# K and V of a head group projected together by token, 160 columns, in a two-block attention kernel

## The chip, the cores and the metric

The kernel runs on one core of a Trainium2 chip. A core has five engines with instruction streams of their own: TensorE (PE in the profile, its weight loads PEld), VectorE (DVE), ScalarE (ACT), GpSimd (POOL) and SyncE (SP), the last of which here only issues DMAs. Matmuls write to PSUM; ACT and DVE move their results to SBUF. The metric is device microseconds for one execution: the median of three runs was 2835.52 us (2830.86 to 2836.12).

## The reference

Four layers follow each other on 2048 tokens of 640 numbers: A, B, A, B, each with a layer norm ahead and a residual around it. Both A layers use the same weights. Layer A is attention in four segments of 512 tokens with a running memory; it has 32 heads of 20.

```python
def _A_ref(x, wq, wk, wv, wo, beta):
    H, Dh, N, L = 32, 20, 4, 512
    q, k, v = x @ wq, x @ wk, x @ wv          # as heads and segments
    phi = lambda t: jnp.where(t > 0, t + 1.0, jnp.exp(t))
    M, z = 0, 0
    for s in range(N):
        logits = einsum('bhqd,bhkd->bhqk', qs, ks) * Dh ** -0.5 + mask   # causal
        a_dot = softmax(logits) @ vs
        pq = phi(qs)
        a_mem = (pq @ M) / (pq @ z + 1e-06)
        o = g * a_mem + (1.0 - g) * a_dot      # g = sigmoid(beta), per head
        pk = phi(ks)
        M = M + einsum('bhld,bhle->bhde', pk, vs)
        z = z + pk.sum(tokens)
    return o @ wo

x = x + _A_ref(_layernorm(x), ...)
x = x + _B_ref(_layernorm(x), ...)
x = x + _A_ref(_layernorm(x), ...)
x = x + _B_ref(_layernorm(x), ...)
```

Layer B is a recurrent attention over 64 steps of 32 tokens. The change does not touch it.

## The kernel before, in words

`layer_A` works through 32 *groups*: four segments n, and in each eight groups G of four heads. A head takes 32 rows or columns of a tile of 128, 20 of them used. For each group:

- `proj_q` and `proj_k` (lines 276 and 295) project by feature: five matmuls, one for each 128 rows of the 640 inputs, with 128 padded weight columns as weights and 512 tokens moving. The result is Q^T or K^T, [128 head rows, 512 tokens]. ACT copies it to SBUF as `a_qT` and `a_kT`; for K it adds `C.krow`, which sets rows 20 and 21 of each head to 1. Those two rows carry the negated row maximum through the second score product.
- `proj_v` (line 306) projects by token: for each of four tiles of 128 tokens five matmuls with the tokens as weights and 80 weight columns moving. ACT copies the result to `vaug`, whose column 20 of each head is 1, so that the sum of the softmax comes out of the same product.
- `s_round` (lines 366 to 375) makes scores with the mask, `a_S`, and DVE takes the negated row maxima `a_nm`. `negmax_rows` (POOL) and `q_with_max` put them into rows 20 and 21 of the next Q^T, `a_q`. `t_round` (407 to 412) makes the transposed scores `a_T` with the maximum already taken off; ACT takes exp to `a_PT`, and POOL zeroes what lies above the diagonal.
- `pv` (424) multiplies the probabilities with `vaug`; ACT copies out `a_osb`; `norm` divides and puts the group's columns into `Onat`.
- `phi_k` (318 to 324), in segments 0 to 2: PE transposes `a_kT` back to tokens (`a_KN`), ACT takes exp (`a_EK`), POOL clips it to 0..1, DVE adds the positive part of `a_KN` from PSUM: `a_phik`. `state` (333 to 353) uses the memory for `a_NUM` in segments 1 to 3 and adds this group's product `a_UP` of `a_phik` and `vaug` to it.
- `out_stage_a` and `out_stage_b` (248 to 265) project finished token tiles of the segment before with `wo` (`a_YP`), in groups 2 to 5 of segments 1 to 3 and after the last group.

The groups are software pipelined: while group g has its scores made, `t_round` works on a group some three half groups behind, `proj_q` and `proj_k` on g + 1, `pv` on g - 2. The loop at the end of `layer_A` says at which (half, round) each piece is called. The framework's scheduler then lays out each engine's stream from that; an engine takes its stream in order.

Two PSUM pools couple the engines. `a_psx` has three buffers for the score tiles `a_S` and `a_T`, each freed by the reduce on DVE or the exp on ACT. `a_pg` has two buffers for everything else: QP, KP, VP, KN, NUM, UP, YP, Q2, PV and the transposes take turns, and each waits for the copy that frees the buffer two tiles before it.

Weights: `load_A_weights` pads `wq` and `wk` from a staging copy in the first A layer, stores the padded forms to DRAM, and the second A layer loads them from there. `wv` is loaded as it is.

Of the kernel before, what the change touches and what calls it, by code (L numbers as in the profile page):

```python
# [28 lines left out]
D = 640  # L29
# [8 lines left out]
def alloc_consts(tc, ctx):  # L38
    cp = ctx.enter_context(tc.tile_pool(name="consts", bufs=1))
    C = Consts()  # L40
    C.pool = cp
    C.identb = cp.tile([128, 128], BF16, name="c_identb")
    C.mhalf = cp.tile([128, 1], F32, name="c_mhalf")
    C.negu = cp.tile([128, 2, 128], BF16, name="c_negu")
    C.krow = cp.tile([128, 1], F32, name="c_krow")
    C.bdmask = cp.tile([128, 128], F32, name="c_bd")
    W = AWeights()
    W.g = cp.tile([128, 32], F32, name="a_g")
    W.omg = cp.tile([128, 32], F32, name="a_omg")
    return C, W  # L50


def build_consts(nc, tc, C):
    with ExitStack() as tctx:
# [15 lines left out]
        krows = tp_.tile([128, 4, 2], F32, name="c_krows")  # L70
        nc.vector.tensor_copy(krows[:], identf[:].rearrange("p (j s) -> p j s", s=32)[:, :, 20:22])
        nc.vector.tensor_reduce(out=C.krow[:], in_=krows[:].rearrange("p j s -> p (j s)"), axis=AX.X, op=ALU.add)
# [68 lines left out]
def load_A_weights(nc, W, A_wq, A_wk, A_wv, A_wo, padded, stage):  # L141

    first = not padded
    for nm, src, pad in (("wq", A_wq, W.wq), ("wk", A_wk, W.wk)):
        if first:
            raw = stage[nm]
            nc.gpsimd.memset(pad[:, :, :, 20:32], 0.0)
            nc.vector.tensor_copy(pad[:, :, :, 0:20], raw.rearrange("p c (h d) -> p c h d", d=20))
        else:
            nc.sync.dma_start(pad[:].rearrange("p c h s -> p (c h s)"), padded[nm])  # L150
    nc.sync.dma_start(W.wv[:], A_wv.rearrange("(c p) n -> p c n", p=128))
    nc.sync.dma_start(W.wo[:], A_wo.rearrange("(c p) n -> p c n", p=128))


def keep_padded(nc, tc, W, padded):
    for nm, pad in (("wq", W.wq), ("wk", W.wk)):
        padded[nm] = tc.dram_tile([128, NCH * 1024], BF16, name=f"a_{nm}_home")
        nc.sync.dma_start(padded[nm], pad[:].rearrange("p c h s -> p (c h s)"))


def layer_A(nc, tc, C, W, x_src, x_dst, src_is_bf16, nseg=4, out_bf16=False, xb_dst=None, load_w=None, side_loads=None):
# [7 lines left out]
    with ExitStack() as ctx:  # L169
# [5 lines left out]
        W.wk = pw.tile([128, NCH, 32, 32], BF16, name="a_wk_pad")  # L175
        W.wv = pw.tile([128, NCH, D], BF16, name="a_wv")
# [28 lines left out]
        vaug = [stm.tile([128, 4, 4, 32], BF16, name=f"a_vaug{i}") for i in range(3)]  # L205
        phik = [ste.tile([128, 4, 4, 32], BF16, name=f"a_phik{i}") for i in range(2)]
        for i in range(3):
            nc.gpsimd.memset(vaug[i][:], 0.0)
            nc.gpsimd.memset(vaug[i][:, :, :, 20:21], 1.0)
# [79 lines left out]
        def proj_k(g):  # L289
            n, G = divmod(g, 8)  # L290
            xnT = SEG[n]["xnT"]
            wkG = W.wk[:, :, 4 * G:4 * G + 4, :].rearrange("p c h s -> p c (h s)")
            KP = pg.tile([128, 512], F32, name="a_KP", tag="pg")
            for c in range(NCH):
                nc.tensor.matmul(KP[:], lhsT=wkG[:, c, :], rhs=xnT[:, c, :], start=(c == 0), stop=(c == NCH - 1))
            kT = qp4.tile([128, 512], BF16, name="a_kT")
            nc.scalar.activation(out=kT[:], in_=KP[:], func=ACT.Identity, bias=C.krow[:, 0:1], scale=1.0)
            GS[g]["kT"] = kT

        def proj_v(g):  # L300
            n, G = divmod(g, 8)
            xnT = SEG[n]["xnT"]
            VP = pg.tile([128, 4, 80], F32, name="a_VP", tag="pg")
            for tt in range(4):
                for c in range(NCH):
                    nc.tensor.matmul(VP[:, tt, :], lhsT=xnT[:, c, 128 * tt:128 * tt + 128], rhs=W.wv[:, c, 80 * G:80 * G + 80],
                                     start=(c == 0), stop=(c == NCH - 1))
            va = vaug[g % 3]
            nc.scalar.copy(va[:, :, :, 0:20], VP[:].rearrange("p t (j s) -> p t j s", s=20))
            GS[g]["va"] = va  # L310

        def phi_k(g):
# [3 lines left out]
            KN = pg.tile([128, 4, 128], BF16, name="a_KN", tag="pg")  # L316
            for tt in range(4):
                nc.tensor.transpose(KN[:, tt, :], GS[g]["kT"][:, 128 * tt:128 * tt + 128], C.identb[:])
            KNv = KN[:].rearrange("p t (j s) -> p t j s", s=32)[:, :, :, 0:20]
# [757 lines left out]
def full_kernel(tc, A_x, A_wq, A_wk, A_wv, A_wo, A_beta, B_x, B_mem0, B_Wq, B_Wk, B_Wv, B_Wo, B_seg_len, out, layers="ABAB"):  # L1077
    nc = tc.nc
    with ExitStack() as ctx:
# [8 lines left out]
        stage = {nm: t_[:, NCH - 1, 0:NCH * D].rearrange("p (c n) -> p c n", c=NCH) for nm, t_ in (("wq", WB.wq), ("wk", WB.wk))}  # L1088
        for nm, src in (("wq", A_wq), ("wk", A_wk)):
# [77 lines left out]
```

## Time and profile before

| what | value |
| --- | --- |
| median of 3 runs | 2835.52 us (2830.86 to 2836.12) |
| the profiled execution's own time | 2836.99 us |
| its span, first to last instruction | 2835.3 us |
| mean granted clock of TensorE | 0.979 |
| first layer A, groups in flight | about 30 to 410 us of the span |
| second layer A, groups in flight | about 1445 to 1830 us |
| PE, DVE, ACT, POOL busy | 2667.9, 1676.5, 1567.3, 702.8 us |

The profile is of one execution. "Busy" is the time in which an engine has an instruction in flight; for PE the ends of matmuls are modelled and hold a pipeline tail, so differences between starts say more than durations. In a line of the timeline the columns are start, duration, engine, source line, operation, output and inputs, shapes, count, and in brackets the idle time before it with what ended it. In a group's line the figures after the bar are busy time and the mean duration of one in ns, then the idle time before it.

### The profile page before, as it was taken

How to read it: one execution, taken by the hardware profiler on the slowest of the kernel's cores; microseconds unless marked ns; L12 is line 12 of the kernel's file. 1: busy time of each engine (PE TensorE's matmuls, PEld its weight loads, DVE VectorE, ACT ScalarE, POOL GpSimd, SP SyncE). 2: the span in 40 equal slices, each digit the busy share in tenths (PEclk: the TensorE clock that was granted, in tenths of full speed). 3: DMA queues.
4: the chain of work that ended last, by engine and by line, in shares of the span. 5: the costliest groups of instructions: out<-in, count | busy, mean ns of one | idle time of the engine just before them, and what ended most of it. 6: DMA issues, size and time to landing. Idle time of an engine off the chain costs nothing.

```text
span 2835.3 us, 147285 instructions
## 1 busy us (share of the span) xinstructions
PE 2667.9 (94%) x65736; PEld 1703.8 (60%) x65736; DVE 1676.5 (59%) x4554; ACT 1567.3 (55%) x3516; POOL 702.8 (25%) x1634
## 2 busy tenths in 40 slices
PE   5899998999999999999979999889999999999998
PEld 2455555666666666666635555556666666666665
DVE  5778864555555555555568878545555555555554
ACT  3777773555555555544448777545555555555443
POOL 3456651111111111111135666411111111111110
PEclk9999999999999999999989999899999999999999
DMA  6110135212221222121130111531211111211110
GB/s 215 53 43 23 39 127 134 44 40 47 44 44 42 43 46 45 41 41 31 31 114 20 57 48 34 174 94 41 43 39 41 41 41 42 43 40 38 39 26 20
DMA packets 322956, 156.54 MB, mean 55 GB/s; under 512 B 245776, under 2 KB 311056, under 8 KB 319248
## 3 DMA queue, kind: packets, MB, share of 16 engines
q1 hardware_dynamic: 320880, 136.63, 19.1%
q8 instruction: 514, 8.42, 1.3%
q10 hardware_dynamic: 1440, 10.49, 1.0%
q14 instruction: 122, 1.00, 0.1%
HBM read 95.65 MB, written 51.38 MB: 52 GB/s over the span
## 4 chain that ended last, share of the span: by engine, by line
PE 54%; DVE 4%; ACT 3%; DMA 2%; issue 1%; POOL 1%; SPq 0%; ACTq 0%; DVEq 0%; POOLq 0%
PE b_OPS L105 7%; PE b_tail L105 4%; PE b_Ka L105 4%; PE b_Qa L105 4%; PE b_Kb L105 4%; PE b_Qb L105 4%; PE b_Va L105 3%; PE b_Vb L105 3%; PE b_SP L105 3%; PE b_OTP L105 2%; PE b_PTP L105 2%; PE b_vtail L105 2%; PE b_OPSd L105 2%; DVE a_nm L375 2%; PE a_QP L276 1%
## 5 line engine op out<-in xcount | busy, mean ns | idle before, releaser
L105 PEld LDWEIGHTS <-b_HX 128*32 128x32 bf16 x15360 | 435.9, 97 | 338.7 <-issue 16.5
L375 DVE TENSOR_REDUCE a_nm<-a_S 128x2 f32<-128x1024 f32 (+3 forms) x512 | 403.7, 811 | 95.1 <-PE a_T L407 71.3
L105 POOL TENSOR_TENSOR b_Pm<-b_E,b_rs 128x96 bf16<-128x96 bf16 x128 | 63.5, 496 | 1446.1 <-ACT b_Vth L105 1082.8
L410 ACT ACTIVATE a_PT<-a_T 128x1024 bf16<-128x1024 f32 (+1 forms) x384 | 340.7, 891 | 51.7 <-PE a_T L407 46.8
L105 PE MATMUL b_OPS<-b_wo,b_OTsb 128*32 128x320 bf16 x8192 | 309.9, 301 | 10.3 <-issue 7.3
L105 PEld LDWEIGHTS <-b_OTsb 128*32 128x32 bf16 x8192 | 201.5, 97 | 97.7 <-DVE b_OTsb L105 25.9
L412 POOL TENSOR_SCALAR_AFFINE_SELECT a_PT<-a_PT 128x256 bf16<-128x256 bf16 (+1 forms) x384 | 198.6, 520 | 235.2 <-ACT a_PT L410 234.0
L105 DVE CAST b_HX<-b_MT 128x8 bf16<-128x8 f32 x372 | 63.7, 172 | 278.5 <-PE b_MT L105 273.4
L105 ACT CAST b_msb<-b_OPS 128x64 bf16<-128x64 f32 x378 | 69.3, 256 | 238.0 <-PE b_OPS L105 238.0
L105 ACT CAST b_kq<-b_Kb 128x512 bf16<-128x512 f32 x128 | 75.0, 586 | 202.4 <-PE b_Kb L105 202.4
L105 DVE COPY b_KT<-b_TPak 128x128 bf16<-128x128 bf16 x128 | 28.8, 225 | 227.2 <-PE b_TPak L105 227.2
L105 PE MATMUL b_Va<-b_wv,b_HX 128*32 128x512 bf16 x2520 | 160.7, 380 | 0.0
L105 PE MATMUL b_Vb<-b_wv,b_HX 128*32 128x512 bf16 x2520 | 160.0, 379 | 0.0
L407 PE MATMUL a_T<-a_q,a_kT 32*128 32x512 bf16 (+3 forms) x1024 | 139.6, 307 | 21.4 <-DVE a_nm L375 14.9
L105 PE MATMUL b_Ka<-b_wk,b_HX 128*32 128x512 bf16 x2520 | 159.0, 379 | 0.0
L105 PE MATMUL b_Kb<-b_wk,b_HX 128*32 128x512 bf16 x2520 | 158.9, 379 | 0.0
L105 PE MATMUL b_Qa<-b_wq,b_HX 128*32 128x512 bf16 x2520 | 158.9, 379 | 0.0
L105 PE MATMUL b_Qb<-b_wq,b_HX 128*32 128x512 bf16 x2520 | 158.9, 379 | 0.0
L105 PEld LDWEIGHTS <-b_kq 128*128 128x128 bf16 x2080 | 116.9, 98 | 69.0 <-ACT b_kq L105 54.8
L105 DVE TENSOR_SCALAR b_kq<-b_Qa 128x512 bf16<-128x512 f32 x128 | 88.5, 692 | 116.7 <-PE b_Qa L105 114.0
L105 DVE CAST b_OTsb<-b_OTP 128x160 bf16<-128x160 f32 (+1 forms) x384 | 122.5, 373 | 40.5 <-PE b_OTP L105 40.3
L105 PE MATMUL b_vtail<-b_wv,b_TX 128*32 128x256 bf16 x2880 | 138.9, 271 | 8.0 <-issue 4.8
(196 smaller groups left out, 5745.1 us busy)
## 6 DMA issues: line engine op xcount, KB each, us to landing
b_QKd<-b_tu SPq DMA_DIRECT2D x128, 128.0 KB
b_tl<-b_QKd SPq DMA_DIRECT2D x128, 128.0 KB
b_wv<-in_B_Wv_dram SPq DMA_DIRECT2D x10, 1024.0 KB
b_wo<-in_B_Wo_dram SPq DMA_DIRECT2D x16, 640.0 KB
b_VTd<-b_vt SPq DMA_DIRECT2D x256, 32.0 KB
b_Vth<-b_VTd SPq DMA_DIRECT2D x512, 16.0 KB
b_XO<-xres SPq DMA_DIRECT2D x256, 30.0 KB
b_wk<-in_B_Wk_dram ACTq DMA_DIRECT2D x5, 1024.0 KB
```

The lines of the kernel that those rows point to most:

```text
L105: r = f(*a, **k)
L276: nc.tensor.matmul(QP[:], lhsT=wqG[:, c, :], rhs=xnT[:, c, :], start=(c == 0), stop=(c == NCH - 1))
L375: nc.vector.tensor_reduce(out=nm[:, qc, 2 * pr:2 * pr + 2], in_=X[:, :, o:o + w_], axis=AX.X, op=ALU.max, negate=True)
L407: nc.tensor.matmul(Y[:, e, o:o + w_], lhsT=kT[rows, 128 * kc:128 * kc + 128], rhs=q2[rows, 128 * kc:512], start=True, stop=True, tile_posi ...
L410: nc.scalar.activation(out=PT[:, :, b:b + width], in_=Y[:, :, 0:width], func=ACT.Exp, scale=SC)
L412: nc.gpsimd.affine_select(out=dv, in_=dv, pattern=[[0, 2], [0, diag], [1, 128]], compare_op=ALU.is_ge, fill=0.0, base=0, channel_multiplie ...
```

## The change

K is no longer projected by feature. `proj_kv` projects K and V of a group by token with one weight tile of 160 columns (80 of K, 80 of V), in two halves of two token tiles each, for the next group. Each half has ten matmuls and two ACT copies: K into `Kn`, a tile of SBUF whose columns 20 and 21 of each head were set to 1 once, and V into `vaug`. `k_turn` makes K^T from `Kn` by four transposes and one ACT copy. `phi_k` no longer transposes K back; it reads `Kn` from SBUF, and is called earlier. V of group g is now made in group g - 1, so `vaug` has a fourth buffer. The weights of K and V are interleaved once, from staged copies on DVE, and stored to DRAM in that form for the second A layer. `C.krow` goes.

```diff
-    nc.sync.dma_start(W.wv[:], A_wv.rearrange("(c p) n -> p c n", p=128))
+    if first:
+        nc.gpsimd.memset(W.wq[:, :, :, 20:32], 0.0)
+        nc.vector.tensor_copy(W.wq[:, :, :, 0:20], stage["wq"].rearrange("p c (h d) -> p c h d", d=20))
+        for i, nm in enumerate(("wk", "wv")):
+            nc.vector.tensor_copy(W.wkv[:, :, :, 80 * i:80 * i + 80], stage[nm].rearrange("p c (g n) -> p c g n", n=80))
+    else:
+        nc.sync.dma_start(W.wq[:].rearrange("p c h s -> p (c h s)"), padded["wq"])
+        nc.sync.dma_start(W.wkv[:].rearrange("p c g n -> p (c g n)"), padded["wkv"])
...
-        vaug = [stm.tile([128, 4, 4, 32], BF16, name=f"a_vaug{i}") for i in range(3)]
+        vaug = [stm.tile([128, 4, 4, 32], BF16, name=f"a_vaug{i}") for i in range(4)]
+        Kn = [stm.tile([128, 4, 4, 32], BF16, name=f"a_Kn{i}") for i in range(2)]
+        for i in range(2):
+            nc.gpsimd.memset(Kn[i][:], 0.0)
+            nc.gpsimd.memset(Kn[i][:, :, :, 20:22], 1.0)
...
-        def proj_k(g):
+        def proj_kv(g, hf):
             n, G = divmod(g, 8)
             xnT = SEG[n]["xnT"]
-            wkG = W.wk[:, :, 4 * G:4 * G + 4, :].rearrange("p c h s -> p c (h s)")
-            KP = pg.tile([128, 512], F32, name="a_KP", tag="pg")
-            for c in range(NCH):
-                nc.tensor.matmul(KP[:], lhsT=wkG[:, c, :], rhs=xnT[:, c, :], start=(c == 0), stop=(c == NCH - 1))
+            KV = pg.tile([128, 2, 160], F32, name="a_KV", tag="pg")
+            for t2 in range(2):
+                tt = 2 * hf + t2
+                for c in range(NCH):
+                    nc.tensor.matmul(KV[:, t2, :], lhsT=xnT[:, c, 128 * tt:128 * tt + 128], rhs=W.wkv[:, c, G, :],
+                                     start=(c == 0), stop=(c == NCH - 1))
+            for dst, o in ((Kn[g % 2], 0), (vaug[g % 4], 80)):
+                nc.scalar.copy(dst[:, 2 * hf:2 * hf + 2, :, 0:20], KV[:, :, o:o + 80].rearrange("p t (j s) -> p t j s", s=20))
+            GS[g]["va"] = vaug[g % 4]
+
+        def k_turn(g):
+            KT_ = pg.tile([128, 4, 128], BF16, name="a_KT", tag="pg")
+            for tt in range(4):
+                nc.tensor.transpose(KT_[:, tt, :], Kn[g % 2][:, tt, :, :].rearrange("p j s -> p (j s)"), C.identb[:])
             kT = qp4.tile([128, 512], BF16, name="a_kT")
-            nc.scalar.activation(out=kT[:], in_=KP[:], func=ACT.Identity, bias=C.krow[:, 0:1], scale=1.0)
+            nc.scalar.copy(kT[:], KT_[:].rearrange("p t k -> p (t k)"))
             GS[g]["kT"] = kT
-
-        def proj_v(g):
-            ...
         def phi_k(g):
             n = g // 8
             if n > nseg - 2:
                 return
-            KN = pg.tile([128, 4, 128], BF16, name="a_KN", tag="pg")
-            for tt in range(4):
-                nc.tensor.transpose(KN[:, tt, :], GS[g]["kT"][:, 128 * tt:128 * tt + 128], C.identb[:])
-            KNv = KN[:].rearrange("p t (j s) -> p t j s", s=32)[:, :, :, 0:20]
+            KNv = Kn[g % 2][:, :, :, 0:20]
...
         proj_q(0)
-        proj_k(0)
+        proj_kv(0, 0)
+        proj_kv(0, 1)
+        k_turn(0)
...
-                    if k == (0, 2) and g + 1 < NGR:
-                        proj_k(g + 1)
-                    if k == (1, 0) and g < NGR:
-                        proj_v(g)
+                    if k == (0, 2):
+                        if g < NGR:
+                            phi_k(g)
+                        if g + 1 < NGR:
+                            proj_kv(g + 1, 0)
+                    if k == (1, 0) and g + 1 < NGR:
+                        proj_kv(g + 1, 1)
                     if k == (1, 1):
                         if 0 <= g - 2 < NGR:
                             pv(g - 2)
-                        if g < NGR:
-                            phi_k(g)
+                        if g + 1 < NGR:
+                            k_turn(g + 1)
...
-        for nm, src in (("wq", A_wq), ("wk", A_wk)):
+        for nm, src in (("wq", A_wq), ("wk", A_wk), ("wv", A_wv)):
             nc.sync.dma_start(stage[nm], src.rearrange("(c p) n -> p c n", p=128))
```

More of the change, by code (lines that the diff above doesn't have):

```diff
@@ L174, in layer_A @@
         W.wq = pw.tile([128, NCH, 32, 32], BF16, name="a_wq_pad")
-        W.wk = pw.tile([128, NCH, 32, 32], BF16, name="a_wk_pad")
-        W.wv = pw.tile([128, NCH, D], BF16, name="a_wv")
+        W.wkv = pw.tile([128, NCH, 8, 160], BF16, name="a_wkv")
         pxT = pool("a_xnT", 2)
```

30 lines of the change are left out of this document (5 added, 25 removed).

## The prediction

> **What bounds the kernel now.** I read the page's table of engines first, then stretches of the two A layers, then the timeline of single groups, then the groups of instructions for prices. In the table TensorE (PE) is the only engine near its span.
>
> ```profile
> PE 2667.9 (94%) x65736; PEld 1703.8 (60%) x65736; DVE 1676.5 (59%) x4554; ACT 1567.3 (55%) x3516; POOL 702.8 (25%) x1634
> ```
>
> The change touches layer A alone, so the second view is busy time by stretch, here the two A layers (columns: stretch, length, busy time of PE, PEld, DVE, ACT, POOL, granted clock, DMA share, GB/s). There PE is busy 300.88 of 325 us, but ACT and DVE stand at 252: three engines hand work round, and the clock is close to full.
>
> ```profile
> core 0: us, PE busy (x) PEld busy (x) DVE busy (x) ACT busy (x) POOL busy (x), PEclk, DMA share, GB/s
> 85.00:410.00 325.00, 300.88 (x3927) 170.02 (x3926) 252.94 (x510) 252.47 (x407) 195.49 (x394) 0.97 0.15 50
> 1425.00:1830.00 405.00, 360.63 (x4626) 205.13 (x4615) 300.84 (x607) 287.55 (x462) 222.16 (x451) 0.94 0.21 66
> ```
>
> The third view is the timeline of one group (four heads) of the second A layer, from its PV block to its Q projection.
>
> ```profile
> 1642.14 1.17 PE L424 MATMUL a_PV<-a_vaug,a_PT 128*128 128x32 bf16 x40
> 1643.15 0.38 PE L318 MATMUL a_KN<-c_identb,a_kT 128*128 128x128 bf16 x4
> 1643.37 0.28 PE L366 MATMUL a_S<-c_negu,c_identb 128*128 128x128 bf16 x2
> ...
> 1643.73 0.44 ACT L321 ACTIVATE a_EK<-a_KN 128x320 f32<-128x320 bf16 x1
> ...
> 1644.26 0.45 POOL L322 TENSOR_SCALAR a_EK<-a_EK 128x320 f32<-128x320 f32 x1 [0.29 <-ACT a_EK L321]
> ...
> 1644.75 0.49 DVE L324 SCALAR_TENSOR_TENSOR a_phik<-a_KN,a_EK 128x320 bf16<-128x320 bf16 x1
> ...
> 1645.30 0.40 PE L348 MATMUL a_UP<-a_vaug,a_phik 128*128 128x128 bf16 x4 [0.19 <-DVE a_phik L324]
> 1645.53 1.24 PE L276 MATMUL a_QP<-a_xnT,a_wq_pad 128*128 128x512 bf16 x5
> ```
>
> See the feature map as a relay: PE transposes K, ACT takes exp, POOL clips, DVE adds, and only then may PE do UP. Busy times of PE hold a modelled pipeline tail, so I count PE by start to start. That of the K and V projections:
>
> ```profile
> 1661.99 1.25 PE L295 MATMUL a_KP<-a_xnT,a_wk_pad 128*128 128x512 bf16 x5
> ...
> 1663.18 0.39 PE L407 MATMUL a_T<-a_q,a_kT 32*128 32x512 bf16 x2
> ...
> 1663.50 0.89 PE L306 MATMUL a_VP<-a_wv,a_xnT 128*128 128x80 bf16 x20
> ...
> 1664.22 0.39 PE L366 MATMUL a_S<-c_negu,c_identb 128*128 128x256 bf16 x2
> ```
>
> KP takes 1.19 us, VP 0.72 (36 ns a matmul), KN 0.22 (1643.15 to 1643.37, 55 ns each). The pace of the groups is read from the same instruction of successive groups:
>
> ```profile
> 1653.91 0.44 ACT L427 COPY a_osb<-a_PV 128x336 f32<-128x336 f32 x1
> 1666.13 0.44 ACT L427 COPY a_osb<-a_PV 128x336 f32<-128x336 f32 x1
> ...
> 1746.69 0.44 ACT L427 COPY a_osb<-a_PV 128x336 f32<-128x336 f32 x1
> 1757.56 0.44 ACT L427 COPY a_osb<-a_PV 128x336 f32<-128x336 f32 x1
> ```
>
> With the one at 1643.40: 10.51 us without an output stage, 12.22 with one (YP), 10.87 in the last segment, where there is no feature map; in segment 0 it is 9.78 (1497.73 to 1507.51).
>
> **PE work, per group.** Removed: KP 1.19, VP 0.72, and KN 0.22 in the 48 groups of segments 0 to 2. Added: 20 matmuls of 160 columns and 4 transposes. No row has 160 columns; 128 take 55 ns (KN), 320 take 0.136 us (YP: 1656.05 to 1656.73, 0.68 for five), so by columns 68 ns, 1.36 us in all, bounds 1.10 and 2.7. The first half stands between row-tiled matmuls like KP and keeps KP's switch of about 0.11 us. KT costs what KN did, 0.22. Balance: 2.13 becomes 1.69, minus 0.44 us; in segment 3, which had no KN, minus 0.22.
>
> Weighed against that: the Trainium skill, "TensorE: Matmul & The Clock Gate", section "Back-to-back issue gap", says that pairs of weight load and matmul sustain about 81 ns at 128 columns and 131 at 512. An estimate between them is 85 ns for 160 columns, 0.34 us more a group, and would make it 22 us over 64 groups: no gain. The trace's 55 and 36 ns speak against it here.
>
> **ACT work.** Prices come from the groups of instructions (busy, mean ns):
>
> ```profile
> L297 ACT ACTIVATE a_kT<-a_KP,c_krow 128x512 bf16<-128x512 f32 x64 | 44.0, 688 | 28.8 <-PE a_KP L295 28.5
> L391 ACT CAST a_q<-a_Q 128x512 bf16<-128x512 f32 x64 | 38.3, 598 | 0.4 <-PE a_Q L388 0.3
> L309 ACT CAST a_vaug<-a_VP 128x320 bf16<-128x320 f32 x64 | 27.3, 427 | 0.7 <-PE a_VP L306 0.6
> L105 ACT CAST b_PTa<-b_PTP 128x160 bf16<-128x160 f32 x256 | 62.3, 295 | 99.8 <-PE b_PTP L105 99.8
> ```
>
> Removed 688 + 427; added four copies of 160 elements at 295 and one kT copy as a_q, 598: 665 ns more a group. But ACT's instructions overlap: two b_PTa back to back take 0.49 us, so one holds ACT 0.19; the others hold it about 0.12 less than their means. So +0.33 us a group, bounds 0.33 and 0.665. EK keeps its price (read from SBUF: no ACT row of this size; I take 443 ns again, bounds plus or minus 0.1, on no path below).
>
> **What moves.** In the changed order KV half 1 stands where KP stood, half 2 where VP stood, KT where KN stood, and UP right behind NUM. EK is done behind the second KV copies, a group ahead, so the relay is off the path. In its place ACT does osb and then the kT copy before UP, YP and the next S. From PV's start (no YP): NUM waits for osb, 1.75 (as now: 1643.89 less 1642.14). kT follows osb's 0.33 of ACT: 1.57 to 2.17, so UP, whose PSUM buffer (two in that pool) is the one KT used, starts at 2.22 instead of 3.16. S 512 follows at 2.66 (now 2.18), T 512 at 2.77, QP at 3.09 instead of 3.39. What is late next: the S reduce on DVE, which now stands behind upm and a_rd and starts at 3.45 instead of 3.21; it frees T's buffer at 4.66, which puts Q2 at 5.05; qT, EQ, exp and q2 on ACT then let KV start at 6.88 instead of 7.20 (1649.34). From KP to PV now 3.32, less 0.42: PV comes again at 9.8 instead of 10.5, minus 0.65 to 0.70. After KV the S reduce sets a floor: S at 1504.22 to PV at 1506.25 is 2.03 us whatever V costs, so V's shorter price is worth nothing.
>
> With YP: QP waits for the first YP to be added on DVE, and that waits for the same S reduce: 5.5 now and after. So only KV's 0.42 is left. Segment 0: T 512 waits for osb, the reciprocal and the S 256 reduce now as then (2.58), UP comes behind it; QP is at 3.47 against 3.39; 0.42 less 0.08 is 0.35. Segment 3: there was no KN in the way, YP now waits for kT (2.22, now 1.75): plus 0.46 against 0.42, nothing with YP; about 0.3 without.
>
> **Starts.** The first S needs 20 matmuls, copies, KT and the kT copy in series instead of KP and kT: cold, at 0.14 us for 160 columns (five 512s took 2.13), 2.7 + 0.3 + 0.6 + 0.6 against 2.1 + 0.7, plus 1.4 us a layer; less V's 0.9 later, which is under the S reduces. In the first layer one more staged weight (0.82 MB) lies ahead of x on SP's queue, and the store of the wide weights (1.64 MB) ahead of x's third tile, at about 0.3 MB/us; but the weight copies now run before x lands: from minus 1 to plus 4, I take plus 1.2. The second layer loads 0.5 MB less; POOL's extra memsets of 2 us lie in its waits there. DVE loses 12 of 490 ns a phik at most: nothing taken. B is unchanged.
>
> **Sum.** 16 groups without YP in segments 1 and 2 at 0.65: 10.4. 16 with YP at 0.42: 6.7. 16 of segment 0 at 0.35: 5.6. Segment 3, 8 at 0.3: 2.4. The last group's V, gone from each tail: 1.4. Together 26.5, less 4.0 for the starts: minus 22.5. The profiled execution took 2836.99 us around its 2835.3 span, 1.5 above the median of 2835.52; against the median, 2813 to 2814.5. I say 2814.
>
> **Rivals.** (1) *More comes back.* Segment 3 is 1.35 us faster than 12.22 though KN and UP are only 0.45 of PE: 0.9 us hang on the relay. If PE's 0.44 (0.22) and the 0.26 that T 512 waits ahead of UP (1644.72 to 1645.30 against 0.32) both return in all groups: 24.6 + 12.5 + 1.4 - 4 = 34, 2801; with the whole 0.9 in 32 groups, 49: 2786. Against it: the S reduces. (2) *ACT becomes the bound, slower.* Place: osb and kT ahead of UP, S and YP. Start to start (four exps of 0.90, two of 0.48, nine others of 0.31 to 0.59) ACT is taken for 8.5 of 10.5 us in a group with a transpose, 8.8 after. If its 2 us of idle time, nearly all waits for PE's Q, don't shrink, each group grows by 0.33: plus 21 plus 4 - 1.4, 2859; it decides against the change once kT is over 0.8 us later than 2.17, that is, if copies into strided K and V rows don't overlap (plus 0.33 more) and exp queues ahead of osb. For it: from 1643.40 to 1646.2 ACT has hardly a gap. A third of it, 0.1 us a group, gives 2845. (3) *Weight loads bound the 160-column matmuls:* at 85 ns instead of 68, plus 0.34 in 64 groups, 2836; the rows of 36 and 55 ns speak against it. (4) *The starts eat it*, if x's later tiles wait out both stores, plus 10 each: 2834.
>
> **Numbers.** Forecast 0.48 (its own range 2804 to 2824), (1) 0.22, (2) 0.18, (3) 0.06, (4) 0.06. The range reaches from 2794, inside (1), to 2845, a third of (2). Within 0.2% (5.7 us, about what this kernel's measurements can tell) lie (3), (4) in part: 0.09; faster 0.73, slower 0.18.
>
> **What would show it.** KV halves of 0.68 to 0.79 us start to start; no idle time ahead of UP from a_phik; osb to osb 9.8, 11.8, 9.4 and 10.9 in the four kinds of group; the first S about 1.5 us later behind QP. It is wrong if PE waits for a_kT ahead of S or UP by over 0.5 us, if KV costs over 0.8 a half, or if the YP groups gain as much as the others.

## The result, and the profile after

The changed kernel takes 2807.69 us, the median of four runs (2805.53 to 2811.1); the kernel before, in four runs beside it, 2833.19 (2826.18 to 2836.12). The ratio is 0.9916, with a 95% interval of 0.99 to 0.9933: 0.8% faster, 25.5 us. The profiled execution took 2809.46 us around a span of 2807.7, at a mean granted clock of 0.984 (2836.99, 2835.3 and 0.979 before).

The table of engines of the changed kernel, and then busy time in the two A layers (columns as before: stretch, length, PE, PEld, DVE, ACT, POOL, granted clock, DMA share, GB/s):

```profile
PE 2637.4 (94%) x65416; PEld 1720.3 (61%) x65480; DVE 1688.6 (60%) x4553; ACT 1589.9 (57%) x3708; POOL 701.5 (25%) x1645
```

```profile
85.00:410.00 325.00, 296.03 (x3858) 182.71 (x3883) 255.13 (x509) 263.03 (x491) 194.42 (x390) 0.97 0.16 54
1425.00:1830.00 405.00, 359.29 (x4836) 224.14 (x4869) 313.64 (x627) 302.44 (x568) 223.85 (x467) 0.96 0.24 76
```

PE lost 30 us of busy time and ACT gained 23. That fits a sum of 25 us, and it says nothing of where the time came from. The pace of the groups tells more, read from the same copy (osb) of successive groups. The timeline of the changed kernel, second A layer; the pairs are segment 0, a YP group, and a group without YP:

```profile
1479.13 0.44 ACT L421 COPY a_osb<-a_PV 128x336 f32<-128x336 f32 x1
1488.16 0.44 ACT L421 COPY a_osb<-a_PV 128x336 f32<-128x336 f32 x1
...
1552.60 0.44 ACT L421 COPY a_osb<-a_PV 128x336 f32<-128x336 f32 x1
1565.09 0.44 ACT L421 COPY a_osb<-a_PV 128x336 f32<-128x336 f32 x1
...
1621.71 0.44 ACT L421 COPY a_osb<-a_PV 128x336 f32<-128x336 f32 x1
1631.66 0.46 ACT L421 COPY a_osb<-a_PV 128x336 f32<-128x336 f32 x1
```

In the steady groups, segment 0 is at 9.03 us (9.78 before), the groups without YP at 9.95 (10.52), and the YP groups at **12.49, longer than the 12.22 of before**. Taken over all 62 intervals from osb to osb of the two layers, and the stretches ahead, between and behind, the two profiled executions differ like this (us, after minus before):

| part | forecast | measured |
|---|---|---|
| segment 0 (12 intervals) | -5.6 | -8.3 |
| segments 1 and 2 without YP (14) | -9.1 (14 at 0.65) | -9.2 |
| iterations (2, 7) and (3, 0), twice | -1.3 (one of each pair a no-YP group) | **-9.4** |
| segments 1 and 2 with YP (16) | -6.7 | **+4.7** |
| segment 3 (16) | -2.4 | +1.2 |
| up to the first osb | +2.6 | **-3.8** |
| from the last osb of A to the first of the next A | +1.4 less 0.7 | -0.8 |
| behind the last osb of the second A | -0.7 | -2.1 |
| sum | -22.5 | -27.7 |

Iterations are numbered (segment, group) as the loop runs; PV and osb belong to the group two earlier, and an interval has the name of the iteration in which it begins. The forecast sum is some 5 us from this one, but three parts miss it by 6 to 11 us each, and in both directions. The experiments are about those.

Two agreements in the table are in part luck. The 14 intervals without YP match the forecast only in their sum: the four at (2, 0) and (2, 1) gained 0.32 to 0.57 us where 0.65 was said, and the eight of segment 1 gave 7.0 of the 9.2 us; why those gained more was not tested. And the granted clock has a part that the table hides. In seven intervals it was 0.75 to 0.96 before and 1.00 after: the four at (2, 7) and (3, 0), both at (0, 2), and (1, 0) of the first layer. Those seven gave 15.8 of the 20.9 us that the 62 intervals lost. One of them is chance: (0, 2) of the first layer took 11.83 us at clock 1.00 in this trace, and 13.3 at 0.87 in the traces of experiments 2, 3, 4, 6, 7 and 10, which are built on the changed kernel.

The experiments ran in three rounds, on three chips, on which the kernel before took 2821 to 2824 us. So totals are compared by their ratio to the kernel before, and parts by the osb intervals, which repeat to about 0.01 us from run to run in most groups where the clock stays at 1.00. In those terms the changed kernel stands at 0.9916.

### The profile page after: what moved, and what is told of

The parts are those of the page before. It is cut to its first block, busy times and chain, and to the rows that moved or that the text cites. A ratio compares the mean times of both kernels' runs of the same rounds, so it can differ in the third digit from the quotient of the medians.

```text
span 2807.7 us, 146964 instructions
## 1 busy us (share of the span) xinstructions
PE 2637.4 (94%) x65416; PEld 1720.3 (61%) x65480; DVE 1688.6 (60%) x4553; ACT 1589.9 (57%) x3708; POOL 701.5 (25%) x1645
## 4 chain that ended last, share of the span: by engine, by line
PE 76%; ACT 8%; DVE 8%; issue 3%; DMA 3%; POOL 2%; SPq 0%; ACTq 0%; POOLq 0%; DVEq 0%
PE b_OPS L101 10%; PE b_tail L101 6%; PE b_Ka L101 5%; PE b_Qb L101 5%; PE b_Kb L101 5%; PE b_Qa L101 5%; PE b_Va L101 5%; PE b_Vb L101 5%; PE b_SP L101 4%; PE b_OTP L101 3%; DVE a_nm L369 3%; ACT a_PT L404 3%; PE b_PTP L101 3%; PE b_OPSd L101 3%; PE b_vtail L101 3%
## 5 line engine op out<-in xcount | busy, mean ns | idle before, releaser
L101 PEld LDWEIGHTS <-b_HX 128*32 128x32 bf16 x15360 | 435.9, 97 | 337.2 <-issue 15.8
L406 POOL TENSOR_SCALAR_AFFINE_SELECT a_PT<-a_PT 128x256 bf16<-128x256 bf16 (+1 forms) x384 | 204.4, 534 | 196.1 <-ACT a_PT L404 195.4
```

Of the source, the lines that this page charges most:

```text
L101: r = f(*a, **k)
L406: nc.gpsimd.affine_select(out=dv, in_=dv, pattern=[[0, 2], [0, diag], [1, 128]], compare_op=ALU.is_ge, fill=0.0, base=0, channel_multiplie ...
```

## Experiment 1 and 2: the 9 us at (2, 7) and (3, 0)

In the kernel before, these two intervals took 12.0 to 12.1 and 11.7 us; after, 9.8 and 9.3, in both layers. The timeline of the kernel before at the first of them (DVE, then PE), and windows of 2 us there:

```profile
1721.55 0.89 DVE L105 BATCH_NORM_STATS2 b_ln_st<-b_xt 128x6 f32<-128x320 bf16 x2 [1.51 <-DMA b_xt<-xres_bf]
1722.35 1.21 DVE L375 TENSOR_REDUCE a_nm<-a_S 128x2 f32<-128x1024 f32 x1
...
1723.61 0.39 PE L407 MATMUL a_T<-a_q,a_kT 32*128 32x128 bf16 x4 [2.06 <-DVE a_nm L375]
...
1727.85 2.31 PE L276 MATMUL a_QP<-a_xnT,a_wq_pad 128*128 128x512 bf16 x5
```

```profile
1722.00:1724.00 2.00, 0.39 (x7) 0.18 (x6) 1.83 (x5) 0.00 (x0) 0.06 (x1) 1.00 0.83 107
1724.00:1726.00 2.00, 1.70 (x45) 1.21 (x44) 1.47 (x3) 1.46 (x2) 1.13 (x2) 0.56 0.61 10
1726.00:1728.00 2.00, 1.77 (x13) 0.90 (x14) 1.76 (x6) 1.03 (x3) 0.63 (x2) 0.50 0.33 1
```

The first layer-norm of layer B stands in DVE's stream in the middle of layer A. DVE waits 1.51 us for its row tile to arrive, the S reduce stands behind it, PE waits 2.06 us for the reduce, and then the granted clock falls to 0.50 and QP takes 2.31 us where it takes 1.25 elsewhere. B's loads may go that early because their tiles lie over buffers of A that are already free. K's and V's weights take 3840 bytes a partition less in the changed kernel, so A's later buffers lie lower against B's tiles, and B's loads stand at the end of A. I had not looked at that. The first run moves B's tiles in the kernel before and leaves K and V alone:

```diff
-        bx = pool("b_x", 1)
-        sml = pool("b_sml", 2)
         kqp = pool("b_kqp", 4)
+        bx = pool("b_x", 1)
+        sml = pool("b_sml", 2)
```

> The kernel before with one edit in layer B: the pool of its K and Q rows is opened ahead of the pool that holds the first layer-norm tiles, so that these tiles lie 4 KB higher in SBUF, over buffers of layer A that come free later. Theory (B's first layer-norms, hoisted into layer A's groups (2,7) and (3,0), cost them): the two periods at 12.0 to 12.1 and 11.7 us in each A layer come to about 9.8 and 9.3 as in the changed kernel, minus 9.4 us in all; the layer-norms come back at the end of A, at most plus 3; total minus 6 to minus 9 against the kernel before. Rival (the changed K and V order itself made those two periods short): they stay at 12.0 and 11.7, the total within 2 us of the kernel before.

It took 0.9972 of the kernel before (0.9959 to 0.9985), some 8 us less. The two intervals became 9.84 and 9.10 in the first layer, 9.86 and 9.11 in the second: minus 9.6 us. The timeline of PE in that run at the same place:

```profile
1714.43 0.39 PE L407 MATMUL a_T<-a_q,a_kT 32*128 32x128 bf16 x4
...
1717.37 1.25 PE L276 MATMUL a_QP<-a_xnT,a_wq_pad 128*128 128x512 bf16 x4
```

No wait ahead of T, and QP at full clock. So a third of the gain of the change can be had without it, by the order of the pools in layer B. The second run is the reverse: the changed kernel with the 3840 bytes put back. It doesn't restore every place, for the fourth `vaug` and the two `Kn` take 3072 bytes more in the pool `a_stm`, and by these sizes what lies behind that pool lies that much higher than before.

```diff
+        pad = pool("a_pad", 1).tile([128, 1920], BF16, name="a_pad")
+        nc.gpsimd.memset(pad[:, 0:1], 0.0)
         pxT = pool("a_xnT", 2)
```

> The changed kernel with one edit: 3840 unused bytes a partition behind A's weights, which is what K's and V's weights take less than before, so that layer A's buffers lie where they lay before and B's first layer-norms may be hoisted again. Theory (the smaller weights moved the buffers, and that alone keeps B's layer-norms out of the groups): the periods at (2,7) and (3,0) go from 9.8 and 9.3 back to 11 to 12, plus 5 to 9 us against the changed kernel, so only 16 to 20 us faster than the kernel before. Rival (the layer-norms are hidden when K is turned rather than projected): same time as the changed kernel, within 2 us.

B's layer-norms did come back into the groups, but hardly their price: the intervals went from 9.82 and 9.27 to 10.03 and 10.25, plus 2.4 us in both layers together, where plus 5 to 9 was expected, and the ratio is 0.9905 (0.9885 to 0.9926), no different from the changed kernel's. The timeline of DVE says why:

```profile
1695.56 0.48 DVE L101 BATCH_NORM_STATS2 b_ln_st<-b_xt 128x6 f32<-128x320 bf16 x1
1695.96 1.20 DVE L371 TENSOR_REDUCE a_nm<-a_S 128x2 f32<-128x1024 f32 x1
1697.08 0.48 DVE L101 BATCH_NORM_STATS2 b_ln_st<-b_xt 128x6 f32<-128x320 bf16 x1
```

The statistics stand there without a wait for their tile, one half ahead of the S reduce and one behind it. So the theory was half right: the layout decides whether B's layer-norm is among A's groups, but what costs 2.3 us an interval is DVE waiting there for a DMA with an S reduce behind it, and the clock that falls behind that wait, not the layer-norm's own work (0.6 us an interval here, with the clock at 1.00).

## Experiment 3, 4 and 6: why the YP groups became longer

The timeline of a YP group of the changed kernel (PV starts at 1642.91), from UP to the S reduce:

```profile
1645.15 0.38 PE L342 MATMUL a_UP<-a_vaug,a_phik 128*128 128x128 bf16 x4
...
1645.92 1.52 PE L258 MATMUL a_YP<-a_wo,a_oT 128*128 128x320 bf16 x10
...
1647.37 0.39 PE L401 MATMUL a_T<-a_q,a_kT 32*128 32x512 bf16 x2
...
1647.80 1.02 ACT L404 ACTIVATE a_PT<-a_T 128x1024 bf16<-128x1024 f32 x1 [1.86 <-PE a_T L401]
...
1648.51 1.24 PE L275 MATMUL a_QP<-a_xnT,a_wq_pad 128*128 128x512 bf16 x4 [0.42 <-DVE a_xr L260]
...
1652.27 0.38 PE L366 MATMUL a_S<-a_kT,a_qT 32*128 32x512 bf16 x1
...
1652.59 0.87 PE L295 MATMUL a_KV<-a_wkv,a_xnT 128*128 128x160 bf16 x10
...
1653.38 0.39 PE L366 MATMUL a_S<-a_kT,a_qT 32*128 32x512 bf16 x1
...
1653.81 2.31 DVE L369 TENSOR_REDUCE a_nm<-a_S 128x2 f32<-128x1024 f32 x2 [1.00 <-PE a_T L401]
```

The same in a YP group of the kernel before (PV at 1652.66):

```profile
1655.23 0.39 PE L407 MATMUL a_T<-a_q,a_kT 32*128 32x512 bf16 x2
...
1656.05 0.84 PE L259 MATMUL a_YP<-a_wo,a_oT 128*128 128x320 bf16 x5
...
1657.04 0.34 PE L372 MATMUL a_S<-a_kT,a_qT 32*128 32x384 bf16 x2
...
1658.14 1.24 PE L276 MATMUL a_QP<-a_xnT,a_wq_pad 128*128 128x512 bf16 x5
...
1661.67 0.39 PE L372 MATMUL a_S<-a_kT,a_qT 32*128 32x512 bf16 x2
```

Three things differ from before: T 512 stands behind all ten YP matmuls (before: ahead of them), so ACT idles 1.86 us; QP still starts 5.6 us behind PV, waiting for DVE's add of the YP rows, and now has S 384 behind it rather than ahead; and one S 512 matmul stands on each side of KV half 1, so the S reduce starts 1.5 us later within the group. Each could be the cause. The first run keeps S 512 whole, by calling half 1 behind it in the YP groups; the second does so in all groups:

```diff
-                        if g + 1 < NGR:
+                        if g + 1 < NGR and not (n >= 1 and 2 <= G <= 5):
                             proj_kv(g + 1, 0)
                     if k == (1, 0) and g + 1 < NGR:
+                        if n >= 1 and 2 <= G <= 5:
+                            proj_kv(g + 1, 0)
                         proj_kv(g + 1, 1)
```

> The changed kernel with KV half 1 called behind the S 512 round in the groups 2 to 5 of a segment, so that both S 512 matmuls stand ahead of it on PE (S 512 x2, KV x7, T 512 x2, KV x13) rather than one on each side. Theory (the split S 512 makes the floor from S through the reduce to PV bind): YP groups of segments 1 and 2 go from 12.49 to 11.8 to 12.2 us, minus 5 to minus 11 us over 16 groups against the changed kernel. Rival (QP's wait for the YP rows to be added on DVE sets these groups): they stay at 12.4 to 12.5, no change within 2 us; if the kT copy comes later by the KV matmuls put behind T 512, plus 2 to 5 us.

> The changed kernel with both KV halves called behind the S 512 round in all groups. Theory (floor from S 512 through the reduce to PV): YP groups gain as in the run before this one; in the other groups S 512 stands up to 0.35 us earlier against KV, and the floor of 2.03 us is not binding there by as much, so minus 0 to minus 0.3 us in 40 groups: minus 5 to minus 18 us in all against the changed kernel. Rival (the K and V copies on ACT, now all behind T 512 and its exp, make kT late): plus 0.2 to 0.5 us a group, slower than the changed kernel by 8 to 25 us.

With S 512 whole the YP groups stood at 12.46 (12.49): the rival, no change. The ratio is 0.9897 (0.9876 to 0.9919). It is not that the reduce didn't start earlier. It did (10.05 against 10.89 us behind PV), but the gain was lost on ACT, where V's and K's copies and EK now come later and stand ahead of exp and osb. ACT's timeline of this run (PV at 1553.99), then of the changed kernel (PV at 1563.83):

```profile
1553.99 0.34 ACT L298 CAST a_vaug<-a_KV 128x160 bf16<-128x160 f32 x1
1554.17 0.51 ACT L315 ACTIVATE a_EK<-a_Kn 128x320 f32<-128x320 bf16 x1
1554.55 1.06 ACT L404 ACTIVATE a_PT<-a_T 128x1024 bf16<-128x1024 f32 x1
1555.45 0.49 ACT L421 COPY a_osb<-a_PV 128x336 f32<-128x336 f32 x1
```

```profile
1563.61 0.49 ACT L315 ACTIVATE a_EK<-a_Kn 128x320 f32<-128x320 bf16 x1
1563.98 1.04 ACT L404 ACTIVATE a_PT<-a_T 128x1024 bf16<-128x1024 f32 x1
1565.09 0.44 ACT L421 COPY a_osb<-a_PV 128x336 f32<-128x336 f32 x1
```

osb starts 1.46 us behind PV instead of 1.26, and all that waits for it (NUM, UP, S 512, the YPs, QP at 5.84 instead of 5.59) with it. Over all 62 intervals the run lost 4.3 us, most of it in segment 3 and at (1, 1) and (2, 1). With both halves behind S 512 everywhere the ratio was 0.9944 (0.9924 to 0.9965): YP groups 12.46 again, and (2, 0) and (2, 1) at 10.4 to 10.5 instead of 10.0 to 10.2. The total is the size of the rival, but not its reason alone: of the 15.5 us that the intervals lost, 9.9 came in five where the granted clock was 0.85 to 0.87, and 1.00 in the changed kernel. The next run tries the late T 512:

```diff
                     k = (half, r)
+                    if k == (0, 0):
+                        n1, G1 = divmod(g - 1, 8)
+                        if 1 <= n1 <= nseg and 2 <= G1 <= 5:
+                            out_stage_b(n1 - 1, G1 - 2)
...
-                        if n >= 1 and 2 <= G <= 5 and n <= nseg:
-                            out_stage_b(n - 1, G - 2)
```

> The changed kernel with the output stage's products (YP) called half a round later, behind the next group's S 512 and T 512 rounds but ahead of QP, so that PE does T 512 ahead of the YPs as the kernel before did. Theory A (T 512 behind ten YP matmuls idles ACT from 3.0 to 4.9 us after PV and delays what follows: this is what the YP groups of segments 1 and 2 lost): 12.49 comes to 12.0 to 12.25, minus 4 to minus 8 us. Theory B (QP's wait for the YP rows to be added on DVE sets the group): 12.4 to 12.6, no change within 3 us.

PE did T 512 ahead of the YPs, and the groups stayed at 12.49 to the digit (ratio 0.9907, 0.9882 to 0.9931). The idle 1.86 us of ACT cost nothing. What is left is QP behind the YPs.

## Experiment 7, 8 and 10: QP ahead of the YPs

```diff
                     if k == (0, 0):
                         if g + 1 < NGR:
                             proj_q(g + 1)
+                        n1, G1 = divmod(g - 1, 8)
+                        if 1 <= n1 <= nseg and 2 <= G1 <= 5:
+                            out_stage_b(n1 - 1, G1 - 2)
```

(with the call at (1, 2) gone, as above)

> The changed kernel with the YP products called behind QP, so that PE does QP right behind T 512 and the YPs after it, and QP waits for no YP row. Theory B (QP's wait for the YP rows on DVE): QP starts at about 3.4 instead of 5.6 us after PV, and the YP groups cost their 1.4 us of PE more than the others: 12.49 becomes 11.3 to 11.7, and YP groups of segment 3 10.97 become 10.3 to 10.9: minus 13 to minus 22 us against the changed kernel. Theory A (late T 512 alone): as the run before, 12.0 to 12.25. A third (the S reduces on DVE set these groups): 12.2 to 12.5.

The YP groups of segments 1 and 2 went to 11.48, inside theory B's range; those of segment 3 went up, 10.97 to 11.53, against it (why is open), for a ratio of 0.9858 (0.9831 to 0.9885). The next-but-one run therefore keeps the move to segments 1 and 2 (`1 <= n1 <= nseg - 2`, and the old place for `n == nseg - 1`):

> The changed kernel with the YP products behind QP in segments 1 and 2 alone; in the last two output stages (segment 3's groups and the tail) they stay where they were, ahead of S 512. Theory: YP groups of segments 1 and 2 at 11.5 as when QP stood ahead everywhere, those of segment 3 back from 11.53 to 10.97, so 3 to 5 us faster than with QP ahead everywhere, and minus 14 to minus 18 us against the changed kernel. Rival (the move in segment 3 was made up elsewhere): same as with QP ahead everywhere within 2 us.

2781.27 us, 0.9847 of the kernel before (0.9826 to 0.9868): the fastest of all runs here, at 11.48 and 10.97, and 14.9 us less than the changed kernel over the intervals of the two layers. Its timeline of PE (PV at 1537.13), then osb to osb:

```profile
1540.13 1.24 PE L275 MATMUL a_QP<-a_xnT,a_wq_pad 128*128 128x512 bf16 x5
1541.20 0.84 PE L258 MATMUL a_YP<-a_wo,a_oT 128*128 128x320 bf16 x5
...
1542.54 0.84 PE L258 MATMUL a_YP<-a_wo,a_oT 128*128 128x320 bf16 x5
```

```profile
1538.38 0.44 ACT L421 COPY a_osb<-a_PV 128x336 f32<-128x336 f32 x1
...
1549.87 0.44 ACT L421 COPY a_osb<-a_PV 128x336 f32<-128x336 f32 x1
```

QP starts 3.00 us behind PV, as in a group without YP, and waits for nothing; a YP group now costs 1.53 us more than one without, little over its own 1.36 us of PE. Between the two runs I also tried to get EK out of osb's way, by giving it upm's buffer:

```diff
-            EK = w1e.tile([128, 4, 4, 20], F32, name="a_EK")
+            EK = w1e.tile([128, 4, 4, 20], F32, name="a_EK", tag="eu")
...
-                upm = w1e.tile([128, 128], F32, name="a_upm")
+                upm = w1e.tile([128, 128], F32, name="a_upm", tag="eu")
```

> As the run before, and EK given the same buffer as upm, so that it may run only after POOL has read upm, some 4 us behind PV, rather than right behind the V copy on ACT. Theory (EK ahead of exp and osb on ACT delays osb, and with it NUM, UP and S 512): 0.1 to 0.3 us less in each of 46 groups with a feature map than the run before, minus 4 to minus 12 us. Rival (exp waits for PE's T 512 anyway): the same within 3 us; or slower, if phik now comes late for UP, which an idle time of PE ahead of UP from phik would show.

1.0089 of the kernel before (1.0065 to 1.0114), some 65 us slower than without the tag; YP groups at 13.40, the others mostly at 10.1 to 12.8. Neither expectation held: it is slower, but PE does not wait for phik ahead of UP, as the rival had it. The list of waits in the second layer (us in total, times, longest) has it, on ACT:

```profile
ACT a_EK L315 <- POOL a_MZ L346: 30.0, 22, 1.7
```

EK kept its early place in ACT's stream and waited there for POOL, 1.4 us a group, with exp and osb behind it. Of the 64.7 us between the intervals of the two runs, 30.4 stand in eleven where the granted clock also fell, to 0.78 to 0.88. The run shows what an ACT that waits costs, with what it does to the clock; whether an EK placed later in that stream would gain stays untried.

## Experiment 5 and 9: what taking the relay off the path is worth

The first of these moves the feature map of the kernel before half a group earlier, and leaves the projections:

```diff
-                    if k == (0, 2) and g + 1 < NGR:
-                        proj_k(g + 1)
+                    if k == (0, 2):
+                        if g < NGR:
+                            phi_k(g)
+                        if g + 1 < NGR:
+                            proj_k(g + 1)
...
-                        if g < NGR:
-                            phi_k(g)
```

> The kernel before with one call moved: the feature map of K (its four transposes, EK, clip, phik) is called at (0, 2), half a group earlier, so that phik is done long before UP; K and V are projected as before. Theory (the relay KN, EK, clip, phik on the path was worth most of the gain): groups without YP in segments 1 and 2 go from 10.52 to 10.0 to 10.3 us, segment 0 from 9.78 to 9.1 to 9.4; the YP groups, where UP now stands ahead of S 512 and both YPs ahead of T 512 as in the changed kernel, do not gain and may lose, 12.2 to 12.8; segment 3 stays at 10.87. Total minus 2 to minus 12 us against the kernel before. Rival (PE's shorter projection is the gain): those groups stay within 0.1 of 10.52 and 9.78, and the YP groups at 12.22.

0.9973 of the kernel before (0.9952 to 0.9994), but not where the theory had it: groups without YP rose to 11.04, YP groups to 12.86, segment 0 stayed at 9.8. QP does start earlier, 2.60 us behind PV instead of 3.39, so the relay is off the path; but the four KN transposes now stand just ahead of S 512, which is split round KP, and from QP to the next PV it takes 8.4 us instead of 7.1. Over the intervals the run lost nothing and gained nothing: 8.0 us less in segment 0, most of it in three intervals where the clock no longer fell, and 4.0 at (2, 7) and (3, 0) stand against 12 more in the rest. The gain is at the start, where the first osb came at 61.0 us instead of 68.1. So on the kernel before, the run doesn't price the relay. The second run prices it on the changed kernel, by putting it back:

```diff
-            KNv = Kn[g % 2][:, :, :, 0:20]
+            KN = pg.tile([128, 4, 128], BF16, name="a_KN", tag="pg")
+            for tt in range(4):
+                nc.tensor.transpose(KN[:, tt, :], GS[g]["kT"][:, 128 * tt:128 * tt + 128], C.identb[:])
+            KNv = KN[:].rearrange("p t (j s) -> p t j s", s=32)[:, :, :, 0:20]
...
                             pv(g - 2)
+                        if g < NGR:
+                            phi_k(g)
```

> The changed kernel with the feature map as before: four transposes of kT into KN behind PV, EK and phik read from KN, while K and V stay projected together. Theory (the relay on the path, and the 0.22 us of transposes, are the larger part of what groups without YP gained): segments 1 and 2 without YP go from 9.95 to 10.2 back to 10.4 to 10.8, segment 0 from 9.04 to 9.4 to 9.8, YP groups from 12.49 to 12.6 to 12.9, segment 3 unchanged, first PV of the first layer 3 to 6 us later: plus 15 to 30 us against the changed kernel. Rival (the shorter K and V products gave it): at most the 0.22 us of the transposes in 48 groups, plus 0 to 11 us.

1.0012 (0.9999 to 1.0025): all of the change's gain was gone. Timeline of ACT, a group without YP (PV at 1640.28); phik and UP in the group itself; and one line of PE's waits in the second layer:

```profile
1641.54 0.44 ACT L424 COPY a_osb<-a_PV 128x336 f32<-128x336 f32 x1
...
1652.13 0.44 ACT L424 COPY a_osb<-a_PV 128x336 f32<-128x336 f32 x1
```

```profile
1642.89 0.49 DVE L321 SCALAR_TENSOR_TENSOR a_phik<-a_KN,a_EK 128x320 bf16<-128x320 bf16 x1
...
1643.44 0.40 PE L345 MATMUL a_UP<-a_vaug,a_phik 128*128 128x128 bf16 x4
```

```profile
PE a_UP L345 <- DVE a_phik L321: 1.6, 5, 0.6
```

10.60 instead of 9.95, segment 0 at 9.94 to 9.96 instead of 9.03, YP groups 12.95 instead of 12.49, segment 3 unchanged: 27.1 us over the intervals of both layers, at the upper end of what was expected, some 6 of it in three intervals of the first layer where the clock fell; only the first osb came less late than said (65.5 us, 64.3 with the change). UP starts 3.16 us behind PV and 0.55 behind phik's start, both as in the kernel before. Few waits for phik show (five of PE in the second layer, 17 before), since PE does half of T 512 in that time. QP starts 3.86 us behind PV instead of 3.00, and from QP to PV little changes (6.74 against 6.84). So a K turned from tokens to columns, plus the transposes back, is no gain at all; the change pays because the feature map reads the tokens as they are, early. How much of that is the relay and how much the 0.22 us of transposes was not separated.

## Experiment 11 and 12: the slack of PE and of ACT

The first does half 2's matmuls twice, into the same place; the second copies V twice:

```diff
-            for t2 in range(2):
+            for t2 in (0, 0, 1, 1) if hf else (0, 1):
```

```diff
-            for dst, o in ((Kn[g % 2], 0), (vaug[g % 4], 80)):
+            for dst, o in ((Kn[g % 2], 0), (vaug[g % 4], 80), (vaug[g % 4], 80)):
```

> The changed kernel with KV half 2's ten matmuls done twice into the same place (the second pass starts the sum anew), 0.70 us of PE work more in each of 64 groups, everything else in the same order on PE. Theory (the floor from S 512 through the S reduce to PV leaves slack behind KV half 2, about 0.2 to 0.35 us): plus 0.35 to 0.5 us a group, plus 22 to 32 us against the changed kernel. Rival 1 (no slack, PE's chain sets every group): plus 0.70 a group, plus 45. Rival 2 (the S reduce alone sets the groups): plus 0.0 to 0.2, under plus 13.

> The changed kernel with the copy of V from PSUM done twice in each half, 0.18 us of ACT occupancy each, 0.37 us a group more, the order on PE kept. Theory (ACT has room; its added copies are hidden behind PE): within plus or minus 6 us of the changed kernel. Rival (ACT sets the groups, or the copies queue ahead of exp and osb): plus 0.2 to 0.37 us a group, plus 13 to 24 us.

Twice half 2: 1.0004 (0.9989 to 1.0019); 0.34 us more in the YP groups, in segment 0 and in the YP groups of segment 3, 0.5 to 0.6 in the groups without YP, 26.9 us over all intervals, as expected by the floor behind S 512, though 6.6 of it stand in two intervals of the first layer where the clock fell. So half 2 has about 0.36 us of slack where S 512 is split or early, and 0.12 in the groups without YP: there the projection is on the path nearly in full. That a shorter one would be worth its length is likely by this, but not shown.

V copied twice: 0.9932 (0.9907 to 0.9957), 7.9 us over the intervals. That is a little over the 6 us that "hidden" allowed, and it is uneven: 0.30 of the added 0.37 us in the YP groups, 0.22 and 0.18 in the others and in segment 0, 0.02 in segment 3. ACT is not the bound, but in groups with a feature map most of what is added between KV half 2 and osb shows. The prediction's rival of ACT as the bound was wrong in its sign, and right about the place.

## Why the prediction was right, and where it was not

- **PE's prices: right.** KV half 1 takes 0.80 us start to start with its switch, half 2 0.70, KT 0.22: 70 ns a matmul of 160 columns, by columns 68 had been said. The Trainium skill, "TensorE: Matmul & The Clock Gate", section "Back-to-back issue gap", would have had some 85 ns by the estimate between its 81 at 128 columns and 131 at 512; the trace disagrees with it here (55 ns at 128, 70 at 160, 215 at 512), and the rival that weight loads bind these products falls.
- **ACT's prices: right.** 1.23 us of copies and 0.60 of kT against the 1.12 taken away is 0.71 (0.665 forecast). EK from SBUF takes 0.49 us, 0.05 more than from PSUM.
- **Groups without YP: right step by step in the steady group, lucky in the sum.** At (2, 0) UP is 2.23 us behind PV (2.22 said), QP 3.00 (3.09), KV 6.81 (6.88), PV again at 9.84 (9.8), and from osb to osb 9.95. Putting the relay back took it all away there, so the reason holds as well. But such groups gained 0.57 at most, not 0.65, and the 9.2 us of all 14 came mostly in segment 1, where the forecast had nothing special.
- **Segment 0: mechanism right, size off.** The mis-sized term is "T 512 waits for osb, the reciprocal and the S 256 reduce now as then (2.58), UP comes behind it; QP is at 3.47". T 512 did start at 2.58, but UP and S 512 stand ahead of it, and QP is at 3.13 against 3.39. With KV's 0.40 that is 0.66 of the 0.75 measured, where 0.35 was forecast. Of the part's 8.3 us, 4.5 came at (0, 2), where the clock fell before, and that was not in the sum.
- **YP groups: wrong, 11 us.** The step that failed is "5.5 now and after. So only KV's 0.42 is left". QP did start at 5.59, for the reason given. But behind QP I took the old order for granted. S 384 moved behind QP, T 256 came 0.45 us later, S 512 by 0.33 and split round KV. The runs show that neither the split nor T 512 makes the length by itself, and that QP ahead of the YPs takes 1.0 us away; which of the smaller shifts behind QP makes up the 0.27 us was not separated.
- **Segment 3: sign wrong, 3.6 us.** YP did wait for kT as forecast (2.23 us behind PV, 1.75 before), and these groups came out at plus 0.10, near the nothing that was said. The 0.3 us for the others did not come: (3, 1) gained 0.10, and (3, 5) and (3, 6) grew by 0.22 and 0.36. No run was made for that.
- **Starts: wrong, 6 us.** The serial K chain was as long as said (4.29 and 4.15 us from KV to the first S, 4.2 said), but what it replaced was mis-sized: 3.72 and 3.92 us instead of 2.8, since four matmuls of the next QP stood there before. So the chain costs 0.6 and 0.2 us, not 1.4 a layer. And the first group of the profile had a wait that I did not look for. The timeline of PE, before and then after:

```profile
42.42 0.37 PE L366 MATMUL a_S<-c_negu,c_identb 128*128 128x128 bf16 x2 [2.24 <-DVE a_nm L375]
...
45.74 0.61 PE L348 MATMUL a_UP<-a_vaug,a_phik 128*128 128x128 bf16 x4 [2.41 <-DVE a_phik L324]
46.14 2.34 PE L276 MATMUL a_QP<-a_xnT,a_wq_pad 128*128 128x512 bf16 x5
```

```profile
39.73 0.39 PE L342 MATMUL a_UP<-a_vaug,a_phik 128*128 128x128 bf16 x4
...
40.83 1.25 PE L275 MATMUL a_QP<-a_xnT,a_wq_pad 128*128 128x512 bf16 x4
```

  phik stood behind five S reduces in DVE's stream, UP waited 2.41 us for it, and QP ran at half the pace. With the feature map called earlier UP comes 6 us sooner. On the kernel before, the run that moved the feature map alone shows that its place is the reason: first osb at 61.0 us. On the changed kernel the feature map put back cost only 1.2 us there (first UP at 40.98), so its late place alone does not bring the wait back; what else keeps phik ahead of the reduces was not separated.
- **Not foreseen: B's layer-norm, 9.4 us,** a side effect of 3840 bytes of SBUF. The first interval of the second layer (12.71 to 9.95) may belong to it too: it fell to 10.15 when only B's tiles were moved.
- **Slips in the sums, without weight:** what one K and V group holds ACT longer comes to 0.36 us from its own terms, not 0.33; 1.19 + 0.72 less 1.36 and 0.11 is 0.44, not 0.42; and the 49 us of the first rival leave out its 1.4.

So the time came out inside the forecast's own range by luck in good part: what was missed, minus 8 at B's layer-norms, minus 6 at the start and minus 3 in segment 0, stands against plus 11 in the YP groups and plus 4 in segment 3. The forecast had no term for the granted clock, and the seven intervals where it fell before hold 15.8 us, more than any of its terms. Of the rivals, "more comes back" had the relay's worth right (0.65 to 0.9 us a group); the slower one did not decide, with kT where it was forecast; and the starts ate nothing.

## What to carry to other kernels

Price a change group by group, in each kind of group, and compare the orders behind the edit as well as at it: an earlier operation that is ready sooner lets a scheduler place others elsewhere, and here that cost more than the saved matmuls in a quarter of the groups. If a change alters a buffer's size, look at what comes to lie where: loads and layer-norms of the next stage may move into or out of the running one, and a DMA wait in an in-order stream stops what stands behind it. Read the granted clock of each interval beside its length: a short wait that tips it costs more than the wait. An engine that is busy 75 to 80% can still be on the path at one point of each group; copies put between a product and the next stage's first copy show there.

## What the runs showed of the hardware that I had not expected

- A wait of 2.06 us was enough for PE's granted clock to fall to 0.50 in the two-microsecond windows from 1724 to 1730 in the kernel before, and it was back at 1.00 by 1732; five 512-column matmuls took 2.11 us start to start in that time and 1.09 elsewhere. The Trainium skill, "TensorE: Matmul & The Clock Gate", in its part on the clock gate, puts the fall behind an idle window of about 3.4 us; the half rate agrees with this trace, the length of the wait here is shorter. Of the 4.6 us that the two intervals of that layer lost, 2.06 was the wait at T; the rest came behind it.
- The clock records of the 14 traces show more of how short a wait can do it. In each trace all steps of the granted clock lie on a grid of 3.41 us, whose place against the program differs from run to run. By the modelled ends of matmuls, and from 60 us on, the clock halved behind all 92 full-clock grid stretches with PE busy under 40%, behind 79 of 193 with 40 to 70%, and behind 8 of some 10,600 above. The stretch with the wait above, 1720.8 to 1724.3, has 40%. So the same waits can cost 1.5 us in one run and nothing in the next: at (0, 2) of the first layer PE waits 1.84 and 0.78 us for the S reduce both in the changed kernel (11.83 us) and in experiment 2 (13.31).
- A copy of 512 elements from bf16 in PSUM (kT, 595 ns) costs ACT as much as one from f32 (q, 598 ns before), and an exp of 320 elements costs 490 ns from SBUF against 443 from PSUM.
- The same kernel before took 2833 us beside the result and 2821 to 2824 in the three rounds of experiments. Steady osb intervals that no edit touched agree to about 0.01 us between the traces, so the difference lies mostly elsewhere, as behind the last osb (1023 to 1026 us in the first two traces, 1010 to 1021 in those of the experiments).
